# An attention and feed-forward block on one core: held-back pieces dealt out between the projections, and the output's multiplication on VectorE

## The chip, the cores and the metric

The kernel runs on one core of one Trainium2 chip. The metric is the time of one execution on the device, in microseconds (us). Below, PE is TensorE (matmuls), DVE is VectorE, ACT is ScalarE, POOL is GpSimd, and SP is SyncE, whose queue here only issues DMAs. Each engine and each queue works through its own list in order.

## The reference

A transformer block whose two halves are modulated by a condition vector, in float32, for x of 2048 × 576:

```python
mod = (_silu(c) @ w_mod).reshape(c.shape[0], 6, 1, -1)
sa, ca, ga, sb, cb, gb = (mod[:, i] for i in range(6))
h = _layernorm(x) * (1 + ca) + sa
x = x + ga * _A_ref(h, A_wqkv, A_wo)     # 32 heads of 18, softmax over 2048 keys, projection wo
h = _layernorm(x) * (1 + cb) + sb
x = x + gb * _B_ref(h, B_w1, B_w2)       # 576 -> 4608, SiLU, 4608 -> 576
```

## The kernel before

**Precision.** Most operands are split into a high part that PE takes exactly and a low remainder, and a product is three matmuls (high·high, high·low, low·high). A contraction over 576 rows (four tiles of 128 and one of 64, KT = 5) so becomes 14 passes.

**Blocks and quads.** After a start that makes q, k and v, the queries go in four blocks of 512 (NQB = 4, numbered 0 to 3 here), the heads in eight quads of four (NQUAD = 8). A quad has 64 slots. In a slot PE makes one tile of scores to find row maxima (psa, L678; DVE takes the maximum, L680), and for a slot some 40 earlier one transposed tile (psb, L725), which ACT turns into exponentials (pt, L727). Every few slots the value matmuls (psv, L762) use them. The maxima of a quad go through a small DRAM buffer into extra rows of q (the DMAs mt to mscr, L705, and mscr to qt, L709).

**The end of a quad** (out_b, L768 to L795): ACT copies the values out of PSUM (ov, L766); DVE transposes them (ou, L780) and takes the reciprocal of the sums (rec, L783). Then the tile is multiplied by it (L785), on POOL in quads 0 to 6 and on DVE in quad 7. DVE transposes it back (ov, L786), and SP moves the rows into the block's output ou (L795).

**The filler.** While PE does the attention of block b+1, the rest of block b is fed in between its slots, in small steps from a list that post(b) fills. In its order: five copies of the output (o_T: ACT makes the high part th, L862; POOL or DVE the low part); the projections proj(0) to proj(3), one for each tile j of 128 rows, whose result is added to the row tile x1[j] (L886 on DVE; L889 on ACT with L890 on POOL for the other half), each followed by its layer norm's statistics (ln_a) and then by ln_c, which applies it (ob, L392); the transposes h_T (psT, L911); the first MLP layer (mlp1, psum tiles from hh, hl and w1t), followed by its SiLU, which leaves g in a high part by ACT (L992) and a low part by POOL (L993); and the second layer (mlp2, from g and w2t).

**Held-back pieces.** The second layer of the last four of the 36 tiles of the hidden dimension is not done with its block. It is cut into 32 pieces (four row tiles j, eight pieces each), kept in the list `left`, and queued with the next block's projections: 16 of them (j = 0 and 1) before proj(0), six after proj(3), then ln_c(3), then the other ten. The last piece of a row tile j adds the result to the old x1[j] and issues its out store (L1011).

**What sets the order.** PE's order is written out by a planner (class Plan) while the kernel is built. It holds a model of time: each PE step, each engine operation, has a cost, and a step may have a `need`, a function that gives the time from which it may go. While a need lies ahead, the planner does attention slots. After the last block it makes no such waits (plan.off). The other engines and the DMA queue are ordered by the scheduler.

**Buffers that tie steps together.** The x1 tiles come from a ring of five. A block takes four, so the new block's x1[1] to x1[3] take buffers that the old block's x1[0] to x1[2] leave; their load (L846) can be issued once the old tile's out store is through. The wo tiles share a ring of four with the w1 tiles, and the fifth wo tile shares one of five with the w2 tiles. Weight loads after block 0 are single DMAs from a DRAM copy (L821). In block 0 the weights are loaded raw, and POOL splits them (L828 to L830).

**The tail.** Block 3 has no attention beside it: its projections, transposes and MLP run alone, with PE's full height.

Of the kernel before, what the change touches and what calls it, by code (L numbers as in the profile page):

```python
# [12 lines left out]
ALU = mybir.AluOpType  # L13
# [5 lines left out]
P = 128  # L19
# [3 lines left out]
DH = 18  # L23
# [8 lines left out]
NQUAD = H // 4  # L32
# [24 lines left out]
END = -4  # L57
END0 = 40
LP0 = 1000
RA, RB = 16, 0  # L60
LP = 8000
PB = 7
QKB = 3
# [20 lines left out]
def f(ap):  # L84
    return ap.bitcast(F32)
# [247 lines left out]
def tile_adaln_block(ctx: ExitStack, tc: tile.TileContext, x, wqkv, wo, w1, w2, c, wfirst, wcol, out):  # L333
    nc = tc.nc
# [81 lines left out]
    plan = Plan()  # L416
    half = {"at": 0}

    def pair_need():
        return plan.when("f", 2)  # L420
# [14 lines left out]
    def chain(ops, t, release=None, last=None):  # L435

        if not ops:
            if last is not None:
                last(t)
            return  # L440

        def done(t):
            if release is not None:
                release(t)
            chain(ops[1:], t + TR, None, last)
        plan.op(ops[0][0], t, ops[0][1], done)
# [172 lines left out]
    o = {}  # L619
# [151 lines left out]
    def out_b(i, ov):  # L771

        b, qd = divmod(i, NQUAD)
        if qd == 0:
            if b:
                fill.until("h_T")
            o[b] = att.tile([P, KT, QB], F32, tag="o", name="ou", bufs=1)
        ou = o[b]
        tt = ou[:, 4, :]
        nc.vector.transpose(tt, ov)  # L780
        blocks = tt.rearrange("p (b c) -> p b c", c=32)
        rec = att.tile([P, 16], F32, name="rec", bufs=2)
        nc.vector.reciprocal(rec, blocks[:, :, DH])  # L783
        eng = nc.vector if qd == NQUAD - 1 else nc.gpsimd
        eng.tensor_tensor(blocks[:, :, :DH], blocks[:, :, :DH], rec[:, :, None].to_broadcast([P, 16, DH]), op=ALU.mult)  # L785
        nc.vector.transpose(ov, tt)  # L786
        chain([("V", 600), ("V", 260), ("V", 800), ("V", 600)], plan.t + 700, None, lambda at: o.update({("at", b): at + 5000}))
        for h in range(4):
            c0 = 72 * qd + DH * h
            while c0 < 72 * qd + DH * h + DH:  # L790
                kt, r0 = divmod(c0, P)
                n = min(72 * qd + DH * h + DH - c0, P - r0)
                p0 = 32 * h + c0 - 72 * qd - DH * h
                for r in (r0, r0 + 64) if kt == 4 else (r0,):
                    nc.sync.dma_start(ou[r:r + n, kt, :], ov[p0:p0 + n, :])  # L795
                c0 += n
        del quads[i]
        if qd == NQUAD - 1:
            post(b)
# [16 lines left out]
    left = []  # L816
# [31 lines left out]
    def post(b):  # L848
        fill.flush()
        pool = mp["p"]  # L850
        fl = fill
        fl.__init__(plan)
        c = ready[b]
        last = state["tail"] = plan.off = b == NQB - 1

        def o_T(kt):
            if kt == 0:
                c["th"] = pool.tile([P, KT, QB], F32R, tag="th", name="th")
                c["tl"] = pool.tile([P, 4, QB], F32R, tag="tl", name="tl")
            hi, src = c["th"][:, kt, :], o[b][:, kt, :]  # L860
            plan.op("A", plan.t, 600)
            nc.scalar.activation(hi, src, AF.Copy)  # L862
            eng = nc.vector if last and kt % 2 == 0 else nc.gpsimd
            if kt < 4:
                eng.tensor_tensor(c["tl"][:, kt, :], src, f(hi), op=ALU.subtract)
            else:
                eng.tensor_tensor(hi[64:], src[64:], f(hi)[64:], op=ALU.subtract)
# [30 lines left out]
        def ln_c(j):  # L898
            mv, rs = c["ln", j]
            if j == 0:  # L900
                c["ob"] = att.tile([P, NST, 640], F32, tag="o", name="ob", bufs=1)
            ln_apply(c["x1"][j], c["ob"][:, j, :], mv[:, 0, :], rs, nc.vector)
# [14 lines left out]
        def rest(n):  # L917
            for _ in range(min(n, len(left))):
                fl.add(*left.pop(0))

        for kt in range(KT):
            fl.add(0, lambda kt=kt: o_T(kt))
        if b == 0:
            fl.add(LP0)
        rest(RA)

        def o_need():
            at = pair_need()
            return None if at is None else max(at, o["at", b])

        for j in range(NST):
            rest(RB if j else 0)
            for part in range(len(GP)):
                fl.add(MMH * len(GP[part]), lambda j=j, part=part: proj(j, part), need={0: pair_need if j else o_need, len(GP) // 2: half_need}.get(part))
                if part == len(GP) // 2 and j:
                    fl.add(0, lambda j=j: ln_c(j - 1))
            fl.add(0, lambda j=j: ln_a(j))
# [30 lines left out]
        def mlp1(i, part):  # L968
            if part == 0:
                def ops(g, k):  # L970
                    kt, a, w = PASS[k]
                    return c["w1", i + g][:, 1 - w, kt * P:(kt + 1) * P], (c["hl"] if a else c["hh"])[:, kt, :]

                c["p1"] = Pair([bank("ps1", psA) for _ in range(2)], ops, 14, not state["tail"])
            for s in GR[part]:
                c["p1"].step(s)
            if part < NG - 1:
                return
            us = c["p1"].ps
            if not state["tail"]:  # L980

                us = [etmp(), etmp()]
                nc.scalar.activation(us[0], c["p1"].ps[0], AF.Copy)  # L983
                nc.vector.tensor_copy(us[1], c["p1"].ps[1])
                for n in range(2):
                    chain([(("A", 600), ("V", 690))[n], ("A", 630), ("V", 690), ("A", 630)], plan.t + 200, c["p1"].release[n])
            for g_ in range(2):
                u, t = us[g_], etmp()
                nc.scalar.activation(t, u, AF.Tanh, scale=0.5)  # L989
                nc.vector.scalar_tensor_tensor(t, t, 1.0, u, op0=ALU.add, op1=ALU.mult)  # L990
                g = pool.tile([P, 2, QB], F32R, tag="g", name="g", bufs=GB)
                nc.scalar.activation(g[:, 0, :], t, AF.Copy)  # L992
                (nc.vector if last else nc.gpsimd).tensor_tensor(g[:, 1, :], t, f(g[:, 0, :]), op=ALU.subtract)  # L993
                c["g", i + g_] = g
# [45 lines left out]
        def add_mlp2(i0, add):  # L1040
            for j in range(NST):
                for part in range(len(G2)):
                    add(MMH * len(G2[part]), lambda j=j, part=part: mlp2(i0, j, part), None, {0: pair_need, len(G2) // 2: half_need}.get(part))
# [10 lines left out]
        if last:  # L1054
            add_mlp2(NFT - CH, fl.add)
        else:
            fl.add(0, lambda: prefetch(b + 1))
            add_mlp2(NFT - CH, lambda *a: left.append(a))
            fl.pace(state["now"], NQUAD * 64 - END)

    def first_part():
# [379 lines left out]
    while now < 2 * (total + LEAD) or pend or later:  # L1441
# [8 lines left out]
        n = kts_ready()  # L1450
# [49 lines left out]
        else:  # L1500
            sa, j = divmod(now, 2)
# [56 lines left out]
```

## Time and profile before

| | us |
|---|---|
| median of 3 runs | 2581.41 (2577.93 to 2584.32) |
| the profiled execution | 2577.16 |
| its span | 2575.4 |
| PE busy | 2409.2 (94%) |
| DVE busy | 1785.8 (69%) |
| ACT busy | 1499.4 (58%) |
| POOL busy | 648.6 (25%) |
| mean granted PE clock | 0.97 |

The program's parts lie at these times in the trace: the start until about 200; attention of block 0 until about 530, alone; blocks 1 to 3 with the filler of the block before beside them, with the projections of the filler at 530 to 640, 1160 to 1270 and 1680 to 1850; the tail from about 2260.

A row of a timeline gives the start, the length, the engine, the line, the operation, out<-in with shapes and the count; in brackets stands how long the engine sat idle before it, and what released it. Rows of several like instructions are drawn together. A row of the waits gives who waited for whom, the sum in us, the number of times and the longest. Line numbers in the profile of before are those of the kernel before; from L785 on the changed kernel's are one lower, from L984 on two or three.

### The profile page before, as it was taken

Reading aid. Unit: us, or ns where it says so; the run is one execution under the profiler, and the core shown is the slowest. Engines: PE = TensorE matmul, PEld = TensorE weight load, DVE = VectorE, ACT = ScalarE, POOL = GpSimd, SP = SyncE. Lnnn points to the kernel's source line nnn. Section 1 sums busy time; section 2 is a strip of 40 time slices with the busy share of each in tenths; the row PEclk is TensorE's granted clock in tenths of the full one; section 3 lists DMA queues with packets and bytes.
Section 4 is the critical chain, followed back from the end, with each engine's and each line's share of the span. In section 5 each row is a group of like instructions: output and inputs, shape, how many; then the busy total and the mean of one; then the engine's idle time right before and its main releaser. Section 6 shows DMA issues by size and latency. Waiting matters only on the chain. (4 is left out here: it accounts for less than half of the span.)

```text
span 2575.4 us, 51091 instructions
## 1 busy us (share of the span) xinstructions
PE 2409.2 (94%) x19952; PEld 1576.6 (61%) x19952; DVE 1785.8 (69%) x3079; ACT 1499.4 (58%) x2736; POOL 648.6 (25%) x794
## 2 busy tenths in 40 slices
PE   6999999987899899998799999998899999997999
PEld 5774444434466665665566666665566666676998
DVE  7778888876777776776677777776677777333333
ACT  5247777764576665665476666665666666732121
POOL 5201111141666655552211111111211111110000
PEclk9999999988899999998899999999999999998999
DMA  7833343351565544553444333442433443225563
GB/s 243 257 127 122 115 121 109 104 172 53 175 208 174 168 154 152 174 170 105 160 149 141 127 125 127 146 147 95 165 126 125 141 147 132 100 94 200 179 213 123
DMA packets 170182, 377.78 MB, mean 147 GB/s; under 512 B 27006, under 2 KB 63262, under 8 KB 169942
## 3 DMA queue, kind: packets, MB, share of 16 engines
q1 hardware_dynamic: 165350, 372.22, 43.1%
q8 instruction: 158, 2.59, 0.4%
q10 hardware_dynamic: 4592, 2.29, 0.4%
q14 instruction: 82, 0.67, 0.1%
HBM read 282.87 MB, written 86.33 MB: 143 GB/s over the span
## 5 line engine op out<-in xcount | busy, mean ns | idle before, releaser
L680 DVE TENSOR_REDUCE mx<-psa 128x1 f32<-128x512 f32 x2048 | 1345.0, 685 | 401.8 <-PE psb L725 266.9
L727 ACT ACTIVATE pt<-psb 128x512 f32<-128x512 f32 x2048 | 1162.0, 598 | 613.0 <-PE psb L725 439.5
L678 PE MATMUL psa<-kt,qt 54*128 54x512 f32 x2048 | 779.1, 430 | 71.5 <-DVE mx L680 66.3
L725 PE MATMUL psb<-qt,kt 56*128 56x512 f32 x2048 | 799.5, 434 | 5.7 <-ACT pt L727 4.1
L678 PEld LDWEIGHTS psa<-kt,qt 54*128 54x128 f32 x2048 | 346.6, 187 | 482.2 <-DVE mx L680 332.3
L762 PE MATMUL psv<-pt,vt 128*32 128x512 f32 x4096 | 544.9, 613 | 0.0
L470 PE MATMUL ps<-w2t,g 64*128 64x288 f32 x4992 | 427.5, 297 | 24.9 <-DVE x L886 11.5
L470 PEld LDWEIGHTS ps<-w2t,g 64*128 64x128 f32 x4992 | 397.1, 189 | 64.4 <-DVE x L886 13.2
L470 PE MATMUL ps<-hh,w1t 64*128 64x512 f32 x2160 | 389.6, 396 | 0.2
L725 PEld LDWEIGHTS psb<-qt,kt 56*128 56x128 f32 x2048 | 350.1, 187 | 38.0 <-ACT pt L727 26.1
L470 PEld LDWEIGHTS ps<-hh,w1t 64*128 64x128 f32 x2160 | 223.1, 186 | 62.0 <-issue 14.7
L993 POOL TENSOR_TENSOR g<-etmp,g 128x512 fp32r<-128x512 f32 x108 | 139.2, 1303 | 361.3 <-ACT g L992 361.3
L890 POOL TENSOR_TENSOR x<-x,gt 128x288 f32<-128x288 f32 x116 | 92.7, 800 | 484.9 <-ACT gt L889 461.2
L762 PEld LDWEIGHTS psv<-pt,vt 128*32 128x32 f32 x4096 | 91.7, 109 | 176.9 <-issue 166.8
L470 PE MATMUL ps<-hl,w1t 64*128 64x512 f32 x864 | 191.1, 394 | 0.0
L886 DVE TENSOR_TENSOR x<-ps,x 128x288 f32<-128x288 f32 x184 | 83.5, 454 | 122.0 <-PE ps L464 79.2
L464 PE MATMUL ps<-w2t,g 128*128 128x288 f32 x960 | 133.0, 299 | 5.2 <-ACT g L992 3.8
L464 PEld LDWEIGHTS ps<-w2t,g 128*128 128x128 f32 x960 | 130.8, 191 | 8.0 <-ACT g L992 4.3
L464 PE MATMUL ps<-hh,w1t 128*128 128x512 f32 x360 | 107.3, 392 | 0.0
L989 ACT ACTIVATE eq<-ps 128x512 f32<-128x512 f32 x36 | 21.6, 600 | 147.1 <-PE ps L464 147.1
L470 PEld LDWEIGHTS ps<-hl,w1t 64*128 64x128 f32 x864 | 95.9, 186 | 15.1
L990 DVE SCALAR_TENSOR_TENSOR etmp<-etmp 128x512 f32<-128x512 f32 x108 | 80.6, 780 | 17.4 <-ACT etmp L989 17.2
(140 smaller groups left out, 2042.5 us busy)
## 6 DMA issues: line engine op xcount, KB each, us to landing
w1t<-w1s SPq DMA_DIRECT2D x108, 640.0 KB
w2t<-w2s SPq DMA_DIRECT2D x108, 576.0 KB
kt<-kscr SPq DMA_DIRECT2D x512, 108.0 KB
w1s<-w1t SPq DMA_DIRECT2D x36, 640.0 KB
w2s<-w2t SPq DMA_DIRECT2D x36, 576.0 KB
vt<-vscr SPq DMA_DIRECT2D x32, 608.0 KB
qt<-qscr SPq DMA_DIRECT2D x128, 108.0 KB
raw<-in_w SPq DMA_DIRECT2D x72, 160.0 KB
```

The source lines that it names most:

```text
L464: mm(self.ps[late], lhsT=lhsT, rhs=rhs, start=(i == 0), stop=(i == self.n - 1))
L470: done = mm(self.ps[g], lhsT=lhsT[rows], rhs=rhs[rows], start=(s == 0), stop=(s == 2 * self.n - 1))
L678: mm(ps, lhsT=t["q"][64 * j:64 * j + 54, hp, stt * P:(stt + 1) * P], rhs=t["k", kc, hp][64 * j:64 * j + 54, :], start=True, stop=True)
L680: return lambda: nc.vector.tensor_reduce(t["mx"][:, 2 * j + hp, stt, kc:kc + 1], ps, axis=AX.X, op=ALU.max)
L725: mm(ps, lhsT=t["k", kt // 4, hp][64 * e:64 * e + 56, kt % 4 * P:(kt % 4 + 1) * P], rhs=t["q"][64 * e:64 * e + 56, hp, :], start=True, sto ...
L727: nc.scalar.activation(t["P"][kt, hp][:, e, :], ps, AF.Exp, scale=SCALE)
L762: mm(t["ps"][32 * h:32 * h + 32, :], lhsT=t["v"][:, c0:c0 + 32], rhs=t["P"][kt, h // 2][:, h % 2, :], start=(kt == 0), stop=(kt == NKT - 1 ...
L886: nc.vector.tensor_add(c["x1"][j][:, hs], ps, c["x1"][j][:, hs])
L890: nc.gpsimd.tensor_add(c["x1"][j][:, hs], c["x1"][j][:, hs], t)
L989: nc.scalar.activation(t, u, AF.Tanh, scale=0.5)
L990: nc.vector.scalar_tensor_tensor(t, t, 1.0, u, op0=ALU.add, op1=ALU.mult)
L993: (nc.vector if last else nc.gpsimd).tensor_tensor(g[:, 1, :], t, f(g[:, 0, :]), op=ALU.subtract)
```

## The change

There are four edits.

1. The multiplication at the end of a quad runs on DVE in all eight quads. The planner's costs for this chain of four operations change with it.
2. The held-back pieces are dealt out by a table: 16 before proj(0), eight (j = 2) between proj(0) and proj(1), and after proj(3) six, ln_c(3), two.
3. The copies o_T get a cost of 1 in place of 0, and the last two a need: the time at which the output's transfers are said to be through.
4. The first held-back piece gets a need: besides its PSUM pair, the time at which the two last g tiles are said to be there (end of the ACT operation plus 1600 ns).

```diff
-RA, RB = 16, 0
+REST = (16, 8, 0, 0)
...
-        eng = nc.vector if qd == NQUAD - 1 else nc.gpsimd
-        eng.tensor_tensor(blocks[:, :, :DH], blocks[:, :, :DH], rec[:, :, None].to_broadcast([P, 16, DH]), op=ALU.mult)
+        nc.vector.tensor_tensor(blocks[:, :, :DH], blocks[:, :, :DH], rec[:, :, None].to_broadcast([P, 16, DH]), op=ALU.mult)
         nc.vector.transpose(ov, tt)
-        chain([("V", 600), ("V", 260), ("V", 800), ("V", 600)], plan.t + 700, None, lambda at: o.update({("at", b): at + 5000}))
+        chain([("V", 700), ("V", 260), ("V", 460), ("V", 700)], plan.t + 700, None, lambda at: o.update({("at", b): at + 5500}))
...
         for kt in range(KT):
-            fl.add(0, lambda kt=kt: o_T(kt))
+            fl.add(1, lambda kt=kt: o_T(kt), need=lambda kt=kt: o["at", b] if kt > 2 else 0)
         if b == 0:
             fl.add(LP0)
-        rest(RA)
...
         for j in range(NST):
-            rest(RB if j else 0)
+            rest(REST[j])
...
+                c["gs"] = []
                 for n in range(2):
-                    chain([(("A", 600), ("V", 690))[n], ("A", 630), ("V", 690), ("A", 630)], plan.t + 200, c["p1"].release[n])
+                    chain([(("A", 600), ("V", 690))[n], ("A", 630), ("V", 690), ("A", 630)], plan.t + 200, c["p1"].release[n], lambda at: c["gs"].append(at + 1600))
...
             add_mlp2(NFT - CH, lambda *a: left.append(a))
+            left[0] = left[0][:3] + (lambda: max(pair_need(), *c["gs"]) if pair_need() is not None and len(c["gs"]) == 2 else None,) + left[0][4:]
```

DVE at the ends of quads in block 0's MLP. `ou<-ou,rec` is the multiplication; here + and - are the two kernels:

```order
 L783 RECIPROCAL rec<-ou 128x16
 L680 TENSOR_REDUCE mx<-psa 128x1 x2
-L786 STREAM_TRANSPOSE ov<-ou 128x512
+L784 TENSOR_TENSOR ou<-ou,rec 128x16x18
+L785 STREAM_TRANSPOSE ov<-ou 128x512
 L680 TENSOR_REDUCE mx<-psa 128x1 x3
```

The multiplication is now an instruction of DVE itself, ahead of the second transpose. On POOL it stood among the weight conversions of block 0, as these rows of the kernel before show:

```order
L993 TENSOR_TENSOR g<-etmp,g 128x512
L830 TENSOR_TENSOR w1t<-raw,w1t 128x320
L993 TENSOR_TENSOR g<-etmp,g 128x512
L785 TENSOR_TENSOR ou<-ou,rec 128x16x18
L829 CAST w1t<-raw 128x320
L828 TENSOR_TENSOR raw<-raw,gb 128x288 x2
```

In the change POOL has no such row.

SP's queue where block 1's projections end. `out<-x` is the store of an old row tile, `x<-in_x` the load of a new one, kt are k tiles of the attention, w1t and w2t weights of the MLP. Before:

```order
L821 DMA w1t<-w1s 128x1280
L821 DMA w2t<-w2s 128x1152
L652 DMA kt_87<-kscr 54x512
L705 DMA mscr<-mt 128x32
L709 DMA qt<-mscr 2x32x32 x2
L1011 DMA out<-x_6385 128x576
L846 DMA x_15084<-in_x 128x576
L821 DMA w2t<-w2s 128x1152 x4
```

In the change:

```order
L1009 DMA out<-x_6397 128x576
L845 DMA x_15084<-in_x 128x576
L652 DMA kt_84<-kscr 54x512
L652 DMA kt_85<-kscr 54x512 x2
L652 DMA kt_86<-kscr 54x512 x2
L652 DMA kt_87<-kscr 54x512 x2
L705 DMA mscr<-mt 128x32
L709 DMA qt<-mscr 2x32x32 x2
L820 DMA w1t<-w1s 128x1280 x4
L820 DMA w2t<-w2s 128x1152 x5
```

The store of the old tile j = 2 and the load of the new x1[3] (x_15084) went ahead of the k tiles and of the pair through mscr; the weight loads went behind that pair.

PE at block 1, from the last mlp1 matmuls to the first held-back piece (ps<-w2t,g). Before:

```order
L470 MATMUL ps_14853<-hh,w1t 128x512
L470 MATMUL ps_14854<-hh,w1t 128x512
L678 MATMUL psa<-kt_92,qt 128x512
L725 MATMUL psb<-qt,kt_83 128x512
L678 MATMUL psa<-kt_92,qt 128x512
L725 MATMUL psb<-qt,kt_82 128x512
L470 MATMUL ps_15110<-w2t,g 128x288
```

In the change, from the last score matmul of those:

```order
L725 MATMUL psb<-qt,kt_82 128x512
L678 MATMUL psa<-kt_92,qt 128x512
L725 MATMUL psb<-qt,kt_82 128x512
L762 MATMUL psv_15116<-pt_2116,vt_2122 32x512 x2
L762 MATMUL psv_15116<-pt_2117,vt_2122 32x512 x2
L678 MATMUL psa<-kt_92,qt 128x512
L725 MATMUL psb<-qt,kt_83 128x512
```

Seven more pairs of score matmuls and eight value matmuls come ahead of the piece. ACT's order at the same place, in the change (th is the copy of o_T, g what the piece waits for):

```order
L861 ACTIVATE th<-ou 128x512 x3
L727 ACTIVATE pt_2117<-psb 128x512
L987 ACTIVATE etmp<-etmp 128x512
L727 ACTIVATE pt_2118<-psb 128x512
L987 ACTIVATE etmp<-etmp 128x512
L727 ACTIVATE pt_2118<-psb 128x512
L990 ACTIVATE g<-etmp 128x512
L861 ACTIVATE th<-ou 128x512
L990 ACTIVATE g<-etmp 128x512
L727 ACTIVATE pt_2119<-psb 128x512 x2
```

The fourth copy still stands ahead of the second g.

## The prediction

> **What bounds the kernel now.** Two rows of the page come first:
>
> ```profile
> span 2575.4 us, 51091 instructions
> PE 2409.2 (94%) x19952; PEld 1576.6 (61%) x19952; DVE 1785.8 (69%) x3079; ACT 1499.4 (58%) x2736; POOL 648.6 (25%) x794
> ```
>
> TensorE (PE) is busy for 94% of the span. An average hides where the other 6% lie, so next comes the table by stretches (columns: stretch and its length, busy us of PE, PEld, DVE, ACT, POOL with counts, granted clock, DMA share, GB/s):
>
> ```profile
> 820.00:1000.00 180.00, 162.37 (x1500) 106.99 (x1500) 123.85 (x198) 107.81 (x195) 100.71 (x142) 0.95 0.49 161
> ...
> 1270.00:1680.00 410.00, 405.79 (x3813) 267.72 (x3812) 314.99 (x516) 277.33 (x508) 65.32 (x66) 1.00 0.40 138
> ```
>
> Between 1270 and 1680 PE has 405.79 of 410 us: nothing is to be had there but by less PE work, and the change adds and removes none. So its worth is in the stalls. The timeline of PE shows the long ones (start, length, row; idle time before it and its releaser in brackets):
>
> ```profile
> 827.53 0.50 PE L678 MATMUL psa<-kt,qt 54*128 54x512 f32 x1 [3.06 <-DVE mx L680]
> 898.60 0.79 PE L678 MATMUL psa<-kt,qt 54*128 54x512 f32 x1 [5.93 <-DVE mx L680]
> 971.38 1.09 PE L470 MATMUL ps<-w2t,g 64*128 64x288 f32 x5 [7.09 <-DVE x L886]
> 1037.39 1.85 PE L470 MATMUL ps<-w2t,g 64*128 64x288 f32 x23 [1.37 <-DVE x L886]
> 1254.19 0.79 PE L678 MATMUL psa<-kt,qt 54*128 54x512 f32 x1 [10.74 <-DVE mx L680]
> 1815.47 0.79 PE L678 MATMUL psa<-kt,qt 54*128 54x512 f32 x1 [8.73 <-DVE mx L680]
> 2335.95 3.89 PE L911 MATMUL psT<-ident,ob 128*128 128x128 f32 x17 [13.96 <-DVE ob L392]
> ```
>
> Four groups follow, one for each thing that the change touches.
>
> **A. Multiplication to VectorE.** The stall that ends at 971.38, seen from DVE and POOL, and all such operations in the run:
>
> ```profile
> 970.27 0.71 DVE L786 STREAM_TRANSPOSE ov<-ou 128x512 f32<-128x512 f32 x1 [7.71 <-POOL ou L785]
> ...
> 968.82 0.79 POOL L828 TENSOR_TENSOR raw<-raw,gb 128x288 f32<-128x288 f32 x1 [3.38 <-DMA raw<-in_w]
> 969.57 0.67 POOL L785 TENSOR_TENSOR ou<-ou,rec 128x288 f32<-128x288 f32 x1
> ...
> L780 DVE STREAM_TRANSPOSE ou<-ov x32: 694/701/714, 217.0 to 2289.3; 128x512 f32<-128x512 f32 x32
> L783 DVE RECIPROCAL rec<-ou x32: 223/234/254, 218.2 to 2290.0; 128x16 f32<-128x16 f32 x32
> L786 DVE STREAM_TRANSPOSE ov<-ou x32: 696/711/714, 219.9 to 2291.1; 128x512 f32<-128x512 f32 x32
> L785 POOL TENSOR_TENSOR ou<-ou,rec x28: 668/674/690, 218.6 to 2231.5; 128x288 f32<-128x288 f32 x28
> L785 DVE TENSOR_TENSOR ou<-ou,rec x4: 458/767/784, 589.3 to 2290.3; 128x288 f32<-128x288 f32 x4
> ...
>   DVE ov L786: 39.5, 20
> ```
>
> DVE's second transpose waits 7.71 us for POOL, whose multiplication stands behind a weight conversion that itself waits for a DMA; DVE's row maxima queue behind the transpose, and PE waits for them. All 28 such waits together are 39.5 us of DVE in 20 cases. On DVE the wait for another engine is gone. The four PE stalls are 3.06 + 5.93 + 7.09 + 1.37 = 17.45 us. After long stalls PE also runs slower (clock 0.95 in 820 to 1000; measured under B at about 2 us a stall): two stalls over 5 us, 4 us. The price: the 28 multiplications come to DVE at 0.458 to 0.784 us each (the row of the four that are there already, where the low end stood beside an idle POOL), so 28 × 0.784 = 22 us of DVE at most. Bounds on the path: 0, since PE was busy through 1270 to 1680 with a DVE busy for 314.99 of 410; 22, if every one delays a row maximum that PE waits for. I take 1, being nearest to that full stretch. POOL loses 28 × 0.674 = 19 us, which nothing waits for. A gives −17.45 − 4 + 1 = **−20.5** (−26 to 0).
>
> The Trainium skill, page "GPSIMD Engine Reference", section 1 "Specifications", speaks against the move: POOL's SBUF interfaces are shared with VectorE, and contend with DVE instructions that have two SBUF inputs, as this multiplication has. The spread of 0.458 to 0.784 agrees with it. By the rule all 28 would cost the upper end, which is the bound of 22 already.
>
> **B. Held-back pieces j=2 between projections 0 and 1 (blocks 1 and 2).** SP's queue and DVE at the end of the projections of block 1, and PE after its stall:
>
> ```profile
> 1235.22 0.32 SPq L705 DMA_DIRECT2D mscr<-mt  x1
> 1245.23 1.38 SPq L709 DMA_DIRECT2D qt<-mscr  x2
> 1246.71 0.37 SPq L1011 DMA_DIRECT2D out<-x  x1
> 1248.90 0.34 SPq L846 DMA_DIRECT2D x<-in_x  x1
> ...
> 1251.87 0.46 DVE L886 TENSOR_TENSOR x<-psp,x 128x288 f32<-128x288 f32 x1 [9.78 <-DMA x<-in_x]
> ...
> 1256.77 0.58 DVE L392 TENSOR_SCALAR ob<-x,mv,rs 128x576 f32<-128x576 f32 x1
> ...
> 1257.37 1.64 PE L470 MATMUL ps<-w2t,g 64*128 64x288 f32 x12
> 1259.16 0.96 PE L470 MATMUL ps<-w2t,g 64*128 64x288 f32 x12
> ...
> 1263.79 1.06 PE L762 MATMUL psv<-pt,vt 128*32 128x512 f32 x8
> ```
>
> The last x1 tile of the new block takes the buffer that the old block's tile j=2 leaves. Its load (1248.90) follows that tile's out store (1246.71), which stands behind a transfer waiting ten microseconds at the head of SP (1235.22 to 1245.23). DVE's add then waits 9.78 us, and PE 10.74. In the changed order (shown above) store and load come ahead of the k loads and of that pair: the load is issued about when projection 1 begins, and the wait goes: −10.74 − 8.73 = −19.5. After the stall twelve matmuls take 1.64 us (1257.37), then 0.96 (1259.16). At that ratio the 5.0 us from 1254.19 to 1259.16 lose 2 us: −4 for the two. What is late next: only eight held-back pieces, not sixteen, cover the last layer norm, which runs 5.5 us from the add (1251.87) to the end of L392 (1257.35). The cover is their 48 matmuls, four times 0.96 us, and a pair of slots, some 4.4 us: I take +1.5 each, +3 (0 to 5). B gives **−20.5** (−23 to −10).
>
> The Trainium skill, "TensorE: Matmul & The Clock Gate", "Part 1: The HAM clock gate", gives half rate after some 3.4 us of idling, and as much busy time to regain full rate: an estimate of 1.7 us for each long stall. The ratio of 1.64 to 0.96 agrees, and so do the 2 us here.
>
> **C. The wait of the first held-back piece for g, and the copies.** The waits of 1100 to 1260, then of 1680 to 1850, then ACT:
>
> ```profile
> PE ps L470 <- ACT g L992: 5.5, 2, 4.2
> PE ps L470 <- POOL g L993: 1.7, 2, 1.2
> ...
> PE ps L470 <- ACT g L992: 4.5, 2, 4.2
> ...
> 1177.05 0.63 ACT L862 ACTIVATE th<-ou 128x512 fp32r<-128x512 f32 x1 [2.03 <-DMA ou<-ov]
> ```
>
> PE waits 5.5 + 1.7 = 7.2 us at block 1, 4.5 + 1.7 = 6.2 at block 2. The new condition brings 14 score matmuls and 8 of values ahead of the piece, work that is only moved. But the copies' own condition does nothing: it is asked while the entry that it reads still holds the end of the quad before, and ACT's order keeps the fourth copy, the one that waits 2.03 us for its DMA, ahead of the second g. Since the exponentials for the drawn-in work stand behind it as well, I take 2 of each, **−4** (0 to −13).
>
> **D. The tail.** DVE, SP and PE before the last block's last layer norm:
>
> ```profile
> 2331.90 0.82 DVE L886 TENSOR_TENSOR x<-psp,x 128x288 f32<-128x288 f32 x2 [9.75 <-DMA x<-in_x]
> ...
> 2324.79 0.33 SPq L846 DMA_DIRECT2D x<-in_x  x1
> ...
> 2315.12 6.54 PE L464 MATMUL ps<-w2t,g 128*128 128x288 f32 x48
> ```
>
> The same load comes too late (issued 2324.79, its add waits 9.75 us), and PE stands 13.96 us. Without it the add follows projection 3 at once; from add to transposes it is 2335.95 − 2331.90 = 4.05 us, and two adds of the last pieces (0.46 each, as at 1251.87) come between: 5.0, against half of the 48 matmuls, 3.27, and three transposes of 0.49. About 1.3 us stay exposed: −13.96 + 1.3, and −1.3 for the 17 transposes at half rate (3.89 us). D gives **−14** (−15 to −8).
>
> **The sum**: −20.5 − 20.5 − 4 − 14 = −59. The profiled execution took 2577.16 us (span 2575.4), 4.25 under the median of 2581.41. So 2577.2 − 59 = 2518.2 on its own time, and **2522** as the median.
>
> **Rivals.**
>
> *R1, the weights become the wait.* The same stretch of the trace and the page give:
>
> ```profile
> DMA packets 1117, 3.69 MB, mean 230 GB/s; under 512 B 260, under 2 KB 260, under 8 KB 1116
> ...
> w1t<-w1s SPq DMA_DIRECT2D x108, 640.0 KB
> w2t<-w2s SPq DMA_DIRECT2D x108, 576.0 KB
> ```
>
> The new order puts four w1t and five w2t loads, 5.44 MB, right behind the pair that held SP for ten microseconds, and halves the work between projection 3 and the first MLP matmul. At the 230 GB/s of 1230 to 1246 the four w1t take 11.1 us; with the hold 21, against a cover of about 11 (1254.19 to 1264.85, the end of the last row under B, holds the transposes and 24 of the 48 piece matmuls, half of it at half rate). That leaves 10 us at each of two boundaries: 2522 + 20 = 2542. For it: the hold is in the trace. Against: it was as long because three megabytes went in front of it, and these now come behind.
>
> *R2, VectorE becomes the bound* (the other side). Each of the 28 output blocks is now one run of DVE work of 0.70 + 0.23 + 0.77 + 0.71 = 2.4 us, and if PE stands for all of it, 28 × 2.4 = 67 us: 2522 + 67 = 2589, slower. It decides from 59/28 = 2.1 us a block. For it is a row where a layer norm on DVE stops PE:
>
> ```profile
> 1206.11 0.50 PE L678 MATMUL psa<-kt,qt 54*128 54x512 f32 x1 [1.91 <-DVE mx L680]
> ```
>
> Against: 1270 to 1680 holds output blocks on DVE, with waits for POOL in them, at 405.79 of 410.
>
> *R3, the condition on g works in full*, since the new work lies ahead of the copies' wait: the 9 us left of C's 13 go too, 2513.
>
> **How the numbers follow.** The forecast has 0.57 (own range 2508 to 2536), R1 0.24, R3 0.10, R2 0.04, and 0.05 is left for A or B doing half of what they should and the weights waiting too. The range 2506 to 2553 leaves out R2 and the far ends. A measurement of this kernel tells 0.3%, some 7.7 us, from no change. R2 alone is slower; of the 0.05 left over, 0.01 is faster, 0.03 the same and 0.01 slower. Faster 0.92, the same 0.03, slower 0.05.
>
> **What would show it.** Right: L786 waits for nothing but DVE's own multiplication; no PE gap over 2 us between 820 and 1040; no DVE row waiting for x<-in_x at the ends of the projections of blocks 1 and 2 and in the tail; multiplications of 0.46 to 0.78 us. R1 would show as PE rows ps<-hh,w1t waiting for DMA after the transposes. C would be right if the rows ps<-w2t,g still wait about 5 us at each boundary behind ACT. The forecast is wrong if the x1 loads still come late, or if gaps of 1 to 2 us behind DVE appear at each output block.

## The result, and the profile after

The changed kernel takes 2502.57 us (median; 2497.57 to 2507.75), where the kernel before took 2579.67 us in the same comparison: a ratio of 0.9704, 95% interval 0.9672 to 0.9737. In a second comparison, with the same program once more, it was 2504.76 against 2578.18 us, 0.9720 (0.9703 to 0.9736). That is 73 to 77 us, against the 59 that were forecast. 2502.57 lies 3.4 us under the low end of the range.

The page of the changed kernel:

```profile
span 2499.1 us, 51105 instructions
PE 2392.5 (96%) x19952; PEld 1568.9 (63%) x19952; DVE 1802.2 (72%) x3107; ACT 1495.2 (60%) x2736; POOL 633.4 (25%) x766
```

PE's busy time fell by 16.7 us with the same 19952 matmuls, so part of the gain is clock and not idle time (the mean granted clock is 0.98, where it was 0.97).

**A.** The stretch of block 0's MLP, and the multiplication as the rows of the tile ou show it (durations in ns: least, median, most):

```profile
820.00:1000.00 180.00, 177.77 (x1689) 116.65 (x1686) 142.34 (x228) 122.87 (x223) 113.87 (x157) 1.00 0.55 183
...
L784 DVE TENSOR_TENSOR ou<-ou,rec x32: 448/460/1550, 221.9 to 2227.1; 128x288 f32<-128x288 f32 x32
```

PE is busy for 177.77 of 180 us at a clock of 1.00; before it was busy for 162.37 at 0.95. The multiplication takes 0.46 us in the median, the low end of the prediction's 0.458 to 0.784. The high end was no bound, though: five of the 32 took 1.45 to 1.55 us, each while POOL made the low part of a g tile (L991).

**B.** SP's queue at the end of block 1's projections:

```profile
1183.94 0.34 SPq L1009 DMA_DIRECT2D out<-x  x1
1186.05 0.33 SPq L845 DMA_DIRECT2D x<-in_x  x1
1186.44 16.00 SPq L652 DMA_DIRECT2D kt<-kscr  x7
1204.67 0.34 SPq L705 DMA_DIRECT2D mscr<-mt  x1
1206.11 1.37 SPq L709 DMA_DIRECT2D qt<-mscr  x2
1207.58 1.93 SPq L820 DMA_DIRECT2D w1t<-w1s  x4
```

The load of the last x1 tile is out at 1186.05, and its add runs at 1207.86 without a wait. The pair through mscr now holds the queue for 1.4 us (1204.67 to 1206.11), not ten, with no weights just ahead of it; the weights follow at 1207.58, and PE waits for none of them. R1 did not come about.

**C, D.** PE's longest gaps at block 1, and the tail's last layer norm:

```profile
1150.34 0.50 PE L678 MATMUL psa<-kt,qt 54*128 54x512 f32 x1 [1.75 <-DVE mx L680]
1152.82 1.28 PE L725 MATMUL psb<-qt,kt 56*128 56x512 f32 x2 [1.98 <-ACT pt L727]
1178.64 0.79 PE L678 MATMUL psa<-kt,qt 54*128 54x512 f32 x1 [2.20 <-DVE mx L680]
...
2259.88 2.08 PE L910 MATMUL psT<-ident,ob 128*128 128x128 f32 x17 [1.10 <-DVE ob L392]
```

The wait for g is gone; no row ps<-w2t,g waits for ACT at either boundary, though the prediction gave such waits of about 5 us as the sign that C is right. Before the held-back piece stand two gaps of 1.75 and 1.98 us instead, the second behind exponentials; that delay the prediction did expect. In the tail 1.10 us are left of 13.96, and the 17 transposes take 2.08 us in place of 3.89.

To see where the time went, the span is cut at the starts of DVE's first transposes of a quad (L780), which stand at like places in both programs. "1.7" is quad 7 of block 1. Idle time is length less PE's busy time. The stretches 1.7 to 2.0 and 2.7 to 3.0 are the boundaries of block 1 and of block 2; "block 1 takes 90.5 us" below means the first of them.

| stretch | before: length (idle) | after: length (idle) | difference |
|---|---|---|---|
| start to 0.6 | 525.9 (31.7) | 528.3 (33.2) | +2.4 |
| 0.6 to 1.0, projections of block 0 | 157.6 (33.9) | 151.9 (32.2) | −5.7 |
| 1.0 to 1.7, MLP of block 0 | 484.6 (22.9) | 462.6 (6.6) | −22.0 |
| 1.7 to 2.0, projections of block 1 | 111.0 (24.9) | 90.5 (8.4) | −20.5 |
| 2.0 to 2.7 | 453.8 (4.1) | 452.5 (3.6) | −1.3 |
| 2.7 to 3.0, projections of block 2 | 104.3 (20.7) | 89.7 (6.5) | −14.6 |
| 3.0 to 3.7 | 451.9 (7.0) | 450.5 (6.5) | −1.4 |
| tail | 286.1 (20.8) | 273.0 (9.6) | −13.1 |

A's stretch and the tail came out near the forecast (−22.0 for −20.5, −13.1 for −14). The projections of blocks 1 and 2 gave 35.1 us where B and C together said 24.5, and at those of block 0, where nothing was forecast, 5.7 us went.

At block 1 the waits for x1 and for g don't account for all of it. DVE's order is another place to look. Here are its rows of one layer norm, that of j = 1 at block 1 in the kernel before; those of j = 0 are the same in kind:

```profile
1212.74 0.21 DVE L373 BATCH_NORM_AGGREGATE mv<-st 128x2 f32<-128x12 f32 x1
1212.98 0.15 DVE L379 TENSOR_SCALAR ve<-mv 128x1 f32<-128x1 f32 x1
1213.80 0.16 DVE L384 TENSOR_TENSOR t<-r 128x1 f32<-128x1 f32 x1 [0.66 <-POOL r L381]
1213.99 0.16 DVE L385 TENSOR_TENSOR t<-t,ve 128x1 f32<-128x1 f32 x1
1214.19 0.15 DVE L386 TENSOR_SCALAR t<-t 128x1 f32<-128x1 f32 x1
1214.38 0.16 DVE L388 TENSOR_TENSOR rs<-r,t 128x1 f32<-128x1 f32 x1
1214.57 0.58 DVE L392 TENSOR_SCALAR ob<-x,mv,rs 128x576 f32<-128x576 f32 x1
```

And the same layer norm in the changed kernel:

```profile
1193.56 0.21 DVE L373 BATCH_NORM_AGGREGATE mv<-st 128x2 f32<-128x12 f32 x1
1193.81 0.15 DVE L379 TENSOR_SCALAR ve<-mv 128x1 f32<-128x1 f32 x1
1193.88 0.68 DVE L680 TENSOR_REDUCE mx<-psa 128x1 f32<-128x512 f32 x1
1194.62 0.16 DVE L384 TENSOR_TENSOR t<-r 128x1 f32<-128x1 f32 x1
1194.81 0.16 DVE L385 TENSOR_TENSOR t<-t,ve 128x1 f32<-128x1 f32 x1
1194.89 0.68 DVE L680 TENSOR_REDUCE mx<-psa 128x1 f32<-128x512 f32 x1
1195.49 0.14 DVE L386 TENSOR_SCALAR t<-t 128x1 f32<-128x1 f32 x1
1195.67 0.16 DVE L388 TENSOR_TENSOR rs<-r,t 128x1 f32<-128x1 f32 x1
1195.87 0.58 DVE L392 TENSOR_SCALAR ob<-x,mv,rs 128x576 f32<-128x576 f32 x1
```

Two row maxima (L680) now stand within the chain, one of them in the 0.66 us in which DVE waited for POOL. PE, which needs the maxima to free its score tiles, had a gap of 1.45 us behind the first form (it ended at 1215.80) and none of 0.3 us behind the second. The scheduler wrote DVE's order when the kernel was built; none of the four edits is about it. Counted in the written order, the row maxima between L373 and L392 for j = 0 to 3 are:

| kernel | block 0 | block 1 | block 2 |
|---|---|---|---|
| before | 0, 2, 0, 1 | 0, 0, 0, 2 | 0, 0, 2, 1 |
| changed | 0, 2, 0, 1 | 0, 2, 2, 2 | 0, 2, 2, 2 |

### The profile page after: what moved, and what is told of

It is laid out like the page before. It is cut to its first block, busy times and chain, and to the rows that moved or that the text cites. A ratio compares the mean times of both kernels' runs of the same rounds, so it can differ in the third digit from the quotient of the medians.

```text
span 2499.1 us, 51105 instructions
## 1 busy us (share of the span) xinstructions
PE 2392.5 (96%) x19952; PEld 1568.9 (63%) x19952; DVE 1802.2 (72%) x3107; ACT 1495.2 (60%) x2736; POOL 633.4 (25%) x766
## 4 chain that ended last, share of the span: by engine, by line
PE 80%; DVE 9%; issue 4%; ACT 3%; DMA 2%; POOL 1%; SPq 1%; ACTq 0%; DVEq 0%; POOLq 0%
PE ps L470 25%; PE psv L762 17%; PE psa L678 13%; PE ps L464 9%; PE psb L725 8%; DVE mx L680 3%; PE psqk L551 3%; PE psv L470 2%; PE psp L470 1%; DVE etmp L988 1%; ACT pt L727 1%; DMA qt<-qscr 1%; ACT etmp L987 1%; PE psv L1213 1%; DVE hh L399 1%
## 5 line engine op out<-in xcount | busy, mean ns | idle before, releaser
L680 DVE TENSOR_REDUCE mx<-psa 128x1 f32<-128x512 f32 x2048 | 1343.7, 685 | 378.8 <-PE psb L725 269.3
L470 PE MATMUL ps<-w2t,g 64*128 64x288 f32 x4992 | 418.6, 295 | 3.6 <-DVE x L885 3.6
L470 PEld LDWEIGHTS ps<-w2t,g 64*128 64x128 f32 x4992 | 391.3, 188 | 38.9 <-issue 10.1
L991 POOL TENSOR_TENSOR g<-etmp,g 128x512 fp32r<-128x512 f32 x108 | 140.2, 1313 | 408.8 <-ACT g L990 408.7
L762 PEld LDWEIGHTS psv<-pt,vt 128*32 128x32 f32 x4096 | 91.2, 109 | 175.7 <-issue 165.0
L885 DVE TENSOR_TENSOR x<-ps,x 128x288 f32<-128x288 f32 x184 | 83.5, 454 | 119.8 <-PE ps L464 74.8
L987 ACT ACTIVATE eq<-ps 128x512 f32<-128x512 f32 x36 | 21.5, 598 | 146.4 <-PE ps L464 146.4
```

What stands on the lines that cost most here:

```text
L470: done = mm(self.ps[g], lhsT=lhsT[rows], rhs=rhs[rows], start=(s == 0), stop=(s == 2 * self.n - 1))
L680: return lambda: nc.vector.tensor_reduce(t["mx"][:, 2 * j + hp, stt, kc:kc + 1], ps, axis=AX.X, op=ALU.max)
L762: mm(t["ps"][32 * h:32 * h + 32, :], lhsT=t["v"][:, c0:c0 + 32], rhs=t["P"][kt, h // 2][:, h % 2, :], start=(kt == 0), stop=(kt == NKT - 1 ...
L885: nc.vector.tensor_add(c["x1"][j][:, hs], ps, c["x1"][j][:, hs])
```

## The experiments

The theory after the first look: the 14 to 18 us by which the gain passed the forecast came from the layer norms' order on DVE, from clock, and at block 0 from chance. Rivals: the condition on g does more than was taken (R3 of the prediction), or the new multiplication and the dealing out of the held-back pieces ("the dealing" below) are worth more by themselves. Stretches are named as in the table above; each run was compared with the kernel before on the same chip.

### One edit undone at a time

The multiplication back on POOL:

```diff
-        nc.vector.tensor_tensor(
+        (nc.vector if qd == NQUAD - 1 else nc.gpsimd).tensor_tensor(
             blocks[:, :, :DH], blocks[:, :, :DH], rec...
```

> The changed kernel (2502.6 us) with one thing undone: the multiplication of quads 0 to 6 is back on POOL, the planner's numbers stay. If the move itself took away the stalls in block 0's MLP, as term A of the prediction says and as the times between quad ends in the two traces suggest (21 us between quad 2 and quad 5 of block 1), this gives about 2502.6 + 21 = 2523, with DVE's second transpose waiting for POOL again between 800 and 1050. If the planner's new costs took them away, by putting other work at those places, it stays at 2503.

Measured: 2531.64 us, 0.9826 (0.9809 to 0.9842), 27 to 29 us over the changed kernel. The stretch 1.0 to 1.7 takes 482.0 us against 462.6, with the waits back (rows of the tile ou):

```profile
  DVE ov L785: 42.2, 20
```

So the move took A's stalls away, and the planner's numbers did not. The rest is elsewhere: 7.8 us at block 0's projections (about as much as two profiles of one program differ there, as shown below), 2.3 and 2.8 us in the stretches 2.0 to 2.7 and 3.0 to 3.7, +4.9 us at block 1 and −4.5 us at block 2. The last two are telling. PE's and POOL's orders are the same there, row for row, as in the changed kernel, and ACT's is but for one step; DVE's maxima within the layer norms are 0, 0, 0, 0 at block 1 and 1, 2, 2, 2 at block 2. So in one program the boundary without maxima inside is longer than in the changed kernel (0, 2, 2, 2), and the one with more is shorter. PE's gaps behind the layer norms of block 1 and of block 2:

```profile
1203.75 0.79 PE L678 MATMUL psa<-kt,qt 54*128 54x512 f32 x1 [2.21 <-DVE mx L680]
1221.83 0.49 PE L678 MATMUL psa<-kt,qt 54*128 54x512 f32 x1 [1.87 <-DVE mx L680]
1232.25 0.49 PE L678 MATMUL psa<-kt,qt 54*128 54x512 f32 x1 [1.59 <-DVE mx L680]
1241.56 0.50 PE L678 MATMUL psa<-kt,qt 54*128 54x512 f32 x1 [1.54 <-DVE mx L680]
...
1749.13 0.49 PE L678 MATMUL psa<-kt,qt 54*128 54x512 f32 x1 [0.60 <-DVE mx L680]
1751.07 0.50 PE L678 MATMUL psa<-kt,qt 54*128 54x512 f32 x1 [0.65 <-DVE mx L680]
1781.89 0.50 PE L678 MATMUL psa<-kt,qt 54*128 54x512 f32 x1 [0.48 <-DVE mx L680]
```

The dealing undone (REST = (16, 0, 0, 0)):

> The changed kernel with the dealing of the held-back pieces undone (16, 0, 0, 0). By the terms B and D of the prediction this costs 20.5 + 14 = 34.5 us: 2537. My theory now is that the dealing also took away waits behind the layer norms of projections 0 to 2 (5.2 us of PE gaps at block 1 before, 3.1 after), and that nothing of the 3 us was paid for the shorter cover of the last one: 34.5 + 3 + 4 = 41, 2544. The load of the last x1 tile should again come late at both boundaries and in the tail.

Measured: 2553.26 us, 0.9909 (0.9886 to 0.9932), 48 to 51 us over the changed kernel, more than either expectation. The waits for x1 are back (PE gaps of 8.51 and 10.39 us at the two boundaries); block 1 takes 103.4, block 2 105.9, the tail 286.5 us. In the profile, of a run of 2545.55 us, that is 12.9 + 16.2 + 13.5 = 42.6 us, with 5.1 us more at block 0's projections, where this program is the same as the changed kernel on every engine.

The condition on g taken off:

```diff
-            left[0] = left[0][:3] + (lambda: max(pair_need(), *c["gs"]) if pair_need() is not None and len(c["gs"]) == 2 else None,) + left[0][4:]
```

> The changed kernel without the condition of the first held-back piece on g. Term C of the prediction took 2 us for each of two boundaries: 2507. My theory now is that the condition is worth more, because with the stall the half clock behind it goes too: at block 1 the gap of 7.2 us before became 3.7, and twelve matmuls no longer run at half rate behind it: 3.5 + 3 at each of two boundaries, 13 us, 2516.

Measured: 2508.19 us, 0.9735 (0.9720 to 0.9749). My new theory fell here. The wait is back in full:

```profile
1157.54 0.85 PE L470 MATMUL ps<-w2t,g 64*128 64x288 f32 x4 [4.26 <-ACT g L990]
1158.89 0.60 PE L470 MATMUL ps<-w2t,g 64*128 64x288 f32 x2 [0.50 <-POOL g L991]
1160.33 0.85 PE L470 MATMUL ps<-w2t,g 64*128 64x288 f32 x4 [0.83 <-ACT g L990]
1162.37 0.61 PE L470 MATMUL ps<-w2t,g 64*128 64x288 f32 x2 [1.19 <-POOL g L991]
```

Yet block 1 takes 91.2 us against 90.5, block 2 90.3 against 89.7. The condition is worth 0.7 us a boundary, which is no more than two profiles of the changed kernel differ there (1.0 and 0.3 us): with it PE idles 2 to 3 us less, and is busy 1.5 to 2.7 us longer for the same number of matmuls. In this profile 8.6 us of the difference lie at block 0's projections, which the edit does not reach.

The edit of the copies undone (cost 0, no need):

> The changed kernel with the edit of the o_T copies undone (cost 0, no need). The prediction held that this edit does nothing: 2503. My theory now: what it moved is VectorE's order. In the changed kernel two row maxima stand between the statistics and the end (L392) of the layer norms of j = 1, 2 and 3 at blocks 1 and 2; without this edit none does, and all four run as one piece on VectorE. The kernel with the multiplication on POOL has both forms, with the same order on PE: 95.4 us with all four as one piece (gaps of 2.2, 1.9, 1.6, 1.5 us), 85.2 us with three of four interleaved. From the 0.4 us gaps of the interleaved ones I expect +1.2 for each of six layer norms, and something for the clock: +7 to +10, 2510 to 2513.

Measured: 2514.48 us, 0.9758 (0.9740 to 0.9776), 9.7 us over the changed kernel in the same comparison (2504.76). Block 1 takes 98.6, block 2 93.8 us. With no row maximum within any of their layer norms, the gaps at block 1 are:

```profile
1178.36 0.50 PE L678 MATMUL psa<-kt,qt 54*128 54x512 f32 x1 [1.76 <-DVE mx L680]
1195.58 0.50 PE L678 MATMUL psa<-kt,qt 54*128 54x512 f32 x1 [1.89 <-DVE mx L680]
1207.57 0.50 PE L678 MATMUL psa<-kt,qt 54*128 54x512 f32 x1 [1.64 <-DVE mx L680]
1216.90 0.49 PE L678 MATMUL psa<-kt,qt 54*128 54x512 f32 x1 [1.55 <-DVE mx L680]
```

As expected of the layer norms, then, and not of an edit that does nothing. PE's order differs a little too in this run, so it shows less strictly than the multiplication on POOL that the layer norms are the cause. The sizes are alike: 8.1 and 4.1 us at the two boundaries, against 4.9 there.

### The same program again

> The changed kernel once more, unaltered, for a second profile of the same program. Between the profile of before and that of the change 5.7 us went at the projections of block 0, where none of the edits was meant to act. With the same order on every engine up to there, the kernel without the dealing took 157.0 us for this stretch against 151.9 in the changed kernel, so I think that it is chance (in which phase the granted clock drops after a gap of 1 to 3 us): this run should give anything from 150 to 160 us there, and stretches without long gaps the same to within 0.5 us. If the 5.7 us belong to the change, it gives 151 to 153.

Measured: 2504.76 us (2502.93 to 2508.03), profiled span 2506.2. Block 0's projections take 159.4 us, more than in the kernel before. All other stretches from 1.0 on agree with the first profile to 1.2 us. The kernels with the dealing undone and without the condition on g, whose orders up to the end of that stretch are those of the changed kernel on every engine, took 157.0 and 160.5. So the 5.7 us lie within what chance gives there. The two profiles of one program part early in that stretch. The changed kernel first, 525 to 565:

```profile
525.00:545.00 20.00, 18.13 (x103) 6.46 (x101) 14.45 (x25) 13.68 (x26) 3.94 (x4) 1.00 0.60 193
545.00:565.00 20.00, 16.14 (x96) 5.46 (x92) 15.40 (x24) 13.67 (x24) 14.52 (x23) 1.00 0.53 180
```

Then the same program again:

```profile
525.00:545.00 20.00, 16.63 (x92) 6.00 (x88) 13.81 (x23) 13.07 (x25) 5.55 (x6) 0.97 0.60 188
545.00:565.00 20.00, 18.04 (x78) 5.62 (x78) 11.61 (x19) 10.31 (x18) 10.88 (x17) 0.69 0.44 145
```

The granted clock after 545 is 1.00 in the one and 0.69 in the other, behind a PE gap of 0.97 us (542.5) and of 1.95 us (540.0), and PE does 96 matmuls there or 78. Between 545 and 555 the clock of the second is 0.50.

### Edits alone

The kernel before with only the multiplication moved:

> The kernel before with the multiplication of all quads on VectorE and nothing else. VectorE's order in the layer norms is that of before, so nothing of their gaps can come in. Term A said 20.5 us, the changed kernel with the multiplication back on POOL lost 29 us. My theory: between quad 0 and quad 7 of block 1 it gains the 21 to 22 us of term A, with 1.5 us more in each of the two stretches without long gaps (2 to 3 us together); the rest of the 29 was chance at block 0's projections and the order of the layer norms. 2578 - 24 = 2554. If the 29 belong to it: 2549.

Measured: 2553.54 us, 0.9919 (0.9896 to 0.9942), 23.0 us under the kernel before. The stretch 1.0 to 1.7 takes 462.2 us (−22.4), the two stretches without long gaps 1.3 and 1.4 us less.

The kernel before with only the dealing:

> The kernel before with the held-back pieces dealt out (16, 8, 0, 0) and nothing else. By terms B and D this gives 34.5 us: 2543. VectorE's order has the layer norms of block 1 as one piece each and those of block 2 with two maxima in three of the four, so the gaps behind them should stay at 1.5 to 2 us at block 1 and fall to 0.5 at block 2. My theory: 19.5 of the two waits for x1, 4 to 6 of clock, 13 in the tail, 3 at block 2: 40 us, 2538. The value of the dealing without the other edits lies between 34.5 and the 50 that the changed kernel lost without it.

Measured: 2537.19 us, 0.9852 (0.9832 to 0.9872), 39.4 us under the kernel before. The tail takes 273.1 us (−13.0), block 1 95.9 (−15.1, its layer norms still in one piece with gaps of 2.20, 1.88, 1.62 and 1.56), block 2 90.0 (−14.3). That profile is of the fastest of the four runs (2529.59), so its stretches add up to more than 39.4. The two edits alone give 23.0 + 39.4 = 62.4 us, and the copies' edit, undone, 9.7 more: 72.1, against 73 to 77 measured for all.

### Prices and conditions by themselves

A second DVE operation beside each multiplication:

```diff
+        nc.vector.tensor_tensor(blocks[:, :, :DH], blocks[:, :, :DH], blocks[:, :, :DH], op=ALU.max)
         nc.vector.tensor_tensor(blocks[:, :, :DH], blocks[:, :, :DH], rec[:, :, None].to_broadcast([P, 16, DH]), op=ALU.mult)
```

> The changed kernel with a second DVE operation of the same shape beside each of the 32 multiplications (the maximum of the tile with itself, two inputs from SBUF, the result the same). If a DVE operation at this place costs the path next to nothing, as the prediction took (1 us for 28), this gives 2503 to 2504. If each stands on the path for its length it costs 32 times 0.77 = 25 us: 2527; half hidden, 2515.

Measured: 2512.44 us, 0.9756 (0.9741 to 0.9770), 8 to 10 us more than the changed kernel, between the two, with PE's order as in the changed kernel. In the stretches 2.0 to 2.7 and 3.0 to 3.7 the seven more operations of 0.40 us cost 2.3 and 2.1 us, 0.3 each: there DVE's time is on the path for most of its length. In 1.0 to 1.7 they cost nothing (461.9 us). The tail is 2.9 us longer. Another 7.2 us come at block 2, whose layer norms went to 0, 0, 0, 0: the gaps behind them are 2.19, 1.87, 1.62 and 1.54 us, and one more of 2.03 us, behind exponentials, is not theirs.

The reciprocal root of the layer norm wholly on POOL:

```diff
-        eng = nc.vector if pool is mp.get("p") else nc.gpsimd
+        eng = nc.gpsimd
```

> The changed kernel with the four small steps of the second layer norm's reciprocal root (L379 to L388) on POOL as well, so that VectorE has only statistics and the last step. PE's order is the same. If the gaps of PE behind layer norms come from VectorE standing in its own chain and waiting for POOL (0.66 us) within it, those of 2 us at j = 0 shrink to under 1 and the total falls by 3 to 6 us: 2497 to 2500. If POOL's chain takes longer and VectorE then stands at L392 for it, the gaps grow instead: 2505 to 2515, most of all in the tail, where nothing runs beside it.

Measured: 2508.46 us, 0.9729 (0.9711 to 0.9746), 3.7 us over the changed kernel in the same comparison. The second branch, by the time: the gap at j = 0 grew from 2.2 us to 2.39 at block 1 and 2.40 at block 2, while the tail, where most was expected, stayed at 272.7 us. Fewer DVE instructions didn't help where it still stands at L392, with the maxima behind it. Where the 3.7 us went the profile doesn't show: it is of the fastest of the four runs (2503.56), with 91.2 and 90.1 us at the boundaries.

A copy condition that works:

```diff
+        o["at", b] = None
         chain([("V", 700), ("V", 260), ("V", 460), ("V", 700)], plan.t + 700, ...
...
-            return None if at is None else max(at, o["at", b])
+            return None if at is None or o["at", b] is None else max(at, o["at", b])
```

> The changed kernel with a copy condition that works: the time of the transfers is set to unknown until the planner has placed the last quad's chain, so that the fourth and fifth copy are held until it has. If ACT's exponentials stood behind those copies' DMA waits, the gaps of 1.4 to 2 us before the first held-back piece at blocks 1 and 2, and those of 4.8 and 4.2 us at the first projection of block 0, shrink: up to 3 + 8 us less, 2492 to 2500. But its VectorE order has the four layer norms of block 1 as one piece each, which by the theory above costs 4 to 5 us: 2498 to 2507 in all. If ACT's order is set by the scheduler's model and not by the planner, the gaps stay, and only the loss is left: 2507.

Measured: 2503.35 us, 0.9714 (0.9697 to 0.9730), even with the changed kernel (2504.76). The gaps at block 0's first projection fell from 4.78 and 4.23 to 2.73 and 1.00 us; at block 1 the gap before the first piece is still 3.23 us. Block 1 with 0, 0, 0, 0 takes 99.0 us, block 2 with 1, 2, 2, 2 takes 86.7.

The same with a copy cost of 0, which has the layer norms of the changed kernel:

> The changed kernel with the working copy condition and a cost of 0 for a copy. Its VectorE order has the layer norms interleaved as in the changed kernel. The kernel with the same condition and a cost of 1 came out even (2503.4), with a block 1 that lost 8.5 us to layer norms in one piece and 2 to 3 us won at block 0 and block 2. So here those 8.5 us should not be lost: 2495 to 2498. If the working condition itself costs something at block 1 (exponentials later), 2500 to 2504.

Measured: 2505.32 us, 0.9725 (0.9709 to 0.9742): a miss. The loss at block 1 is gone (90.8 us), as expected, but nothing is won. Block 2 takes 90.1, and block 0's projections 160.1, near the top of what chance gives there. In this program PE waits for g again (4.17 and 4.22 us), with the boundaries as long as without that wait, as in the kernel without the condition.

### A faster one

The changed kernel with two numbers of the planner altered:

```diff
-            fl.add(1, lambda kt=kt: o_T(kt), need=...
+            fl.add(40, lambda kt=kt: o_T(kt), need=...
...
-                    ... lambda at: c["gs"].append(at + 1600))
+                    ... lambda at: c["gs"].append(at + 2400))
```

> The changed kernel with two numbers of the planner altered: cost of a copy 40 in place of 1, g's margin 2400 in place of 1600. VectorE's order then has row maxima within the layer norms of j = 1, 2, 3 at block 0 too (2, 2, 5 in place of 2, 0, 1), and at block 2 within all four; the work is the same. By the theory of the layer norms that is three more interleaved, 1.2 to 1.7 us each: 4 to 5 us under the changed kernel, 2498 to 2500. If the interleaving is not the cause, 2503.

Measured: 2491.39 us (2490.38 to 2492.17), 0.9671 (0.9654 to 0.9687). The four times lie 5 us and more under the fastest of eight of the changed kernel (2497.57), some 12 us under its medians. DVE's counts are 0, 2, 2, 5 at block 0, then 0, 2, 2, 1 and 2, 2, 2, 1. Block 0's gaps behind the layer norms, in this kernel:

```profile
623.78 0.49 PE L678 MATMUL psa<-kt,qt 54*128 54x512 f32 x1 [0.56 <-DVE t L386]
632.82 0.49 PE L678 MATMUL psa<-kt,qt 54*128 54x512 f32 x1 [0.37 <-DVE mx L680]
643.38 0.49 PE L678 MATMUL psa<-kt,qt 54*128 54x512 f32 x1 [0.54 <-DVE mx L680]
647.65 0.49 PE L678 MATMUL psa<-kt,qt 54*128 54x512 f32 x1 [1.27 <-DVE mx L680]
```

And in the changed kernel at the same places:

```profile
619.97 0.50 PE L678 MATMUL psa<-kt,qt 54*128 54x512 f32 x1 [1.13 <-DVE t L386]
631.53 0.50 PE L678 MATMUL psa<-kt,qt 54*128 54x512 f32 x1 [1.88 <-DVE mx L680]
643.65 0.79 PE L678 MATMUL psa<-kt,qt 54*128 54x512 f32 x1 [2.44 <-DVE mx L680]
647.77 0.79 PE L678 MATMUL psa<-kt,qt 54*128 54x512 f32 x1 [3.33 <-DVE mx L680]
```

The stretch takes 148.9 us. In the two kernels with 2, 2 and 5 or 6 there (this one and the one with the doubled operation, 149.9) it is shorter than in all others (151.9 to 160.5). The direction is as the theory had it, the gain more than twice as large as expected, and not all of it is the layer norms'. Against the two profiles of the changed kernel that stretch gives 3.1 or 10.5 us. The two numbers also move PE's work: the boundaries have 50 matmuls fewer (732 for 782) and take 84.8 and 81.2 us, and the stretches behind them have them instead and take 458.7 and 456.5. A boundary and the stretch behind it together are 0.5 us longer at block 1, where the counts are 0, 2, 2, 1, and 2.5 us shorter at block 2. Which part is the gaps, which the clock behind them and which the moved work was not measured apart.

## Why the prediction was too small

- **A, "the four PE stalls are 17.45 us", "two stalls over 5 us, 4 us": right in sum.** The move alone gave 22.4 us in that stretch, against 21.5 for these terms. **The price, "I take 1": wrong in sign.** The argument was that a full stretch hides the multiplication. It did not hide it, since a DVE operation there costs most of its length (0.3 of 0.40 us), nor had it hidden the wait for POOL: the move took 1.3 and 1.4 us off the two full stretches.
- **B, the wait for x1: right**, both waits went, and the order of SP did it. **"What is late next ... I take +1.5 each, +3": did not come.** The last layer norm of block 1 ends at 1212.65 with no PE gap over 0.5 us. The size was not wrong for a layer norm in one piece: where the last one had no maxima inside, the gap behind it was 1.54 to 1.56 us, whatever the other edits. In the changed kernel it has two inside. The step asked whether enough PE work lies beside the chain, and not what stands within the chain on DVE.
- **The clock behind the stalls, 2 us each: right at the stalls, but not the whole.** In the kernel before, the granted clock was 0.50 for the 4.8 us behind block 1's stall (1254.19 to 1259.00) and for the 3.2 us behind block 2's (1815.47 to 1818.70): an estimate of 2.4 and 1.6 us lost. With the dealing alone PE's busy time fell by more, by 5.6 us at block 1 and by 3.4 at block 2 (86.1 to 80.5, 83.5 to 80.1). At block 1 the clock before was 0.50 at 1208 to 1211 and at 1228.5 to 1231.5 too, behind gaps of 1.91 and 1.86 us; with the dealing alone gaps of 1.56 to 2.20 us stand at the like places, and the clock there is 1.00. The prediction had no term for this. The Trainium skill, "TensorE: Matmul & The Clock Gate", "Part 1: The HAM clock gate", from which 1.7 us a stall was estimated, says that the window over which PE's activity is judged runs free; by that rule the price of one stall varies with its phase. These gaps and the 7.5 us between two profiles of one program fit that; the 3.4 us of idling that the prediction took from the same place came before neither the drops at 1208 and 1228.5 nor the one at 545.
- **C, "the copies' own condition does nothing": right of the condition, and the step that failed.** C gave the whole edit of the copies no time for that reason. The fourth copy does still wait for its DMA ahead of the second g, for 1.39 us at block 1, as C said. But the edit moved the order of DVE's layer norms, and undoing it costs 9.7 us, the largest piece of the 14 us or more that the sum lacks. The working followed the edit to PE and ACT; DVE's order at the boundaries, which stood in the two programs, was not read. **The condition on g, "I take 2 of each": too much**, 0.7 each.
- **D: right.** −13.1 us for −14, 1.10 us left for "about 1.3".
- **The sum**: A and its side effects 23.0 for 20.5, B with D 39.4 for 34.5, the copies and the condition some 11 for 4, in all 73 for 59. R1 (PE waits for no weights), R2 (not slower) and R3 (the condition is worth 1.4 us, not 9 more) were all wrong.

What stays open: why work drawn ahead of the first piece shortens the boundary so little though PE idles less, what makes the scheduler put maxima into one layer norm's chain and not into another, and what the copies' edit would do without the others. No run sets DVE's order by itself; the boundaries where PE's order is the same and DVE's is not are the nearest to that.

## What to carry to other kernels

When an edit changes the numbers of a planner or the place of a step, compare the written order of every engine at every in-order chain that waits for another engine, not only where the edit acts, and look whether other work stands within the chain. At blocks 1 and 2, in all fourteen profiles, PE's longest gap behind a layer norm was 1.4 to 2.4 us where no row maximum stood within its chain, and 0.7 us or less where one or two did, apart from the layer norms that had to wait for x1. Among the variants of the changed kernel with the same number of matmuls there, five boundaries without any maxima inside took 4.1, 4.9, 7.2, 8.1 and 8.5 us more than the changed kernel's, with its three layer norms of two maxima, and two boundaries with one more in the first layer norm took 3.0 and 4.5 us less; a part of this is clock. The two conditions that the edits were about gave less. A transfer that waits at the head of a queue holds everything behind it: the small round trip through DRAM held SP's queue for 10.0 us with weight loads issued just ahead of it, and for 1.4 us with the weights behind it. Profile one program twice before a difference of a few us in one stretch is explained.

## What the runs showed of the hardware

- Half clock without a long gap: behind a PE gap of 1.95 us the granted clock was 0.50 from 545 to 555 and 0.69 on average over 20 us, in a stretch where DVE releases PE every 3.5 us or more, while in another run of the same program, behind a gap of 0.97 us, it was 1.00. Over the whole stretch one program took 151.9 and 159.4 us.
- The multiplication on VectorE took 0.77 us in the median of four in the kernel before, and 0.46 us in the median of 32 in the changed one. Three of those four and the five of 1.45 to 1.55 us among the 32 had a POOL operation with two inputs beside them; so had some of the short ones.
